# Windowed attention and a gated MLP on one core: q and k by head pair in every batch, token order restored on the read side, V by a plain load and a cast on GpSimd

## The chip, the cores and the metric

The kernel runs on one core of one Trainium2 chip. The metric is device time in microseconds. The engines are named as in the profile: PE (TensorE matmul; PEld is its weight load), DVE (VectorE), ACT (ScalarE), POOL (GpSimd) and SP (SyncE, which here only issues DMAs). SPq, ACTq and POOLq are the sequencers that issue DMAs.

## The reference

Four batches of 8 heads, 768 tokens, head size 64. Attention looks at a causal window of 96 tokens and at the first 8 tokens, with a bias per head that grows with the distance. Its output, as 3072 rows of 512, goes through a SoLU MLP with a layer norm whose scale is `g_ln`.

```python
def attn(q, k, v, n_global, n_local):            # [4, 8, 768, 64], 8, 96
    scores = matmul(q, k.transpose(0, 1, 3, 2)) / sqrt(64)
    rel = pos[:, None] - pos[None, :]
    is_global = pos[None, :] < n_global
    is_local = (rel >= 0) & (rel < n_local)
    dist = where(is_global & ~is_local, n_local, abs(rel))
    scores = where(is_global | is_local, scores - slopes[h] * dist, -1e9)
    return matmul(softmax(scores), v)

def moe(x, w_in, w_out, g_ln):                   # x [3072, 512], d_ff 1024
    h = x @ w_in
    solu = h * softmax(h)
    ln = (solu - mean(solu)) / sqrt(var(solu) + 1e-6) * g_ln
    return ln @ w_out
```

## The kernel before

The 3072 rows are 24 tiles of 128 tokens, six to a batch. One hand-written loop over t = 0 to 28 sets the order of everything, and each engine executes its share of it strictly in that order. In step t the attention of tile t is made, its two head halves as `scores` (PE into PSUM, exp on ACT), `mask_mul` (DVE) and `av` (PE); `norm` (DVE) of tile t-1 ends in `x16`, which PE transposes and DVE copies to `xT`; the MLP of tile t-2 is made up to `u` (PE `ffn_in`, ACT exp, DVE product, then a DMA transpose of `u` issued by SP), ACT squares it, and GpSimd works out the layer-norm statistics for two tiles at a time; `ffn_out` of tile t-4 runs on PE, and ACT scales and stores tile t-5. So the product u of tile n is made in step n+2, and its start marks that step in the trace.

PSUM is full and nothing in it is double-buffered: the tags are s (scores), av, h (`ph`), o (`po`) and t, which the transposes of x, q and k share.

The scores need q and k with the head size on the partitions, so PE transposes them, and the result is copied from PSUM to `qkT` (fp16, one buffer per batch, two buffers).

Batch 0 comes tile by tile: `load_tile0` loads q, k and v of 128 tokens in rows of 256 B, `cast_tile0` casts q and k on ACT and v on GpSimd, and `fill_tile` transposes eight 128x128 blocks and copies them on DVE at L175. This happens inside the loop, in step t for tile t+1. `cast_tile0` also issues the loads of the weights `w_in` (L83) and `w_out` (L85) from GpSimd.

Batches 1 to 3 come by head pair: `load_pair` loads two heads of q or k of the whole batch in rows of 1536 B, which puts six successive tokens on each partition; `cast_pair` casts on GpSimd; `fill_pair` makes six transposes, whose PSUM result has the tokens in the order (a, t) with token = 6t + a. The DVE copy at L188 reads that in order and scatters it on the write side: successive elements of a partition are written 12 B apart. A list FILLS says in which step each of the 8 fills of a batch is made: the last step or steps before the batch that needs them. In batches 1 and 2 the six steps have 2, 1, 1, 2, 1 and 1 fills; in batch 0 they have 0, 0, 1, 2, 2 and 3.

V of batches 1 to 3 comes by DMAs that GpSimd issues and that cast on the way (`load_v`, L91).

The loads of the pairs and the transposes of u are issued by SP, in program order: a load that waits for a free `raw` buffer (8 of them, released by `cast_pair`) holds up the transposes behind it.

The output weights are centred once: `gw_round` (8 ACT instructions) in step 2, then 8 matmuls for a mean and 8 DVE instructions (`gw_centre`, L361) in step 3.

Of the kernel before, what the change touches and what calls it, by code (L numbers as in the profile page):

```python
# [20 lines left out]
def kernel(  # L21
# [45 lines left out]
    st0 = {}  # L67

    def load_tile0(a):
        t = sb.tile([P, 3, H, D], FP32, name="st0", bufs=3)  # L70
        for w, src in enumerate((q, k, v)):
            nc.sync.dma_start(out=t[:, w],
                              in_=src[0, :, ts(a, P), :].rearrange("h p d -> p h d"))
        st0[a] = t

    def cast_tile0(a):
        t = st0.pop(a)
        qk = sb.tile([P, 2, H, D], FP16, name="qk0")
        nc.scalar.copy(out=qk.rearrange("p w h d -> p (w h d)"),  # L79
                       in_=t[:, 0:2].rearrange("p w h d -> p (w h d)"))  # L80
        nc.gpsimd.tensor_copy(out=vo[:, 0, a, :, 0:D], in_=t[:, 2])
        if a == 0:
            nc.gpsimd.dma_start(out=w_in_sb, in_=moe_w_in.rearrange("(j p) f -> p j f", p=P))  # L83
        if a == 1:
            nc.gpsimd.dma_start(out=w_out32,  # L85
                                in_=moe_w_out.rearrange("(j p) c -> p j c", p=P))
            nc.gpsimd.dma_start(out=g_sb, in_=moe_g_ln.rearrange("(j p) -> p j", p=P))
        return qk

    def load_v(b, a):  # L90
        nc.gpsimd.dma_start(out=vo[:, b, a, :, 0:D],  # L91
                            in_=v[b, :, ts(a, P), :].rearrange("h p d -> p h d"))
# [17 lines left out]
    with tc.manual_schedule():  # L110
        for a in range(3):
            load_tile0(a)
# [42 lines left out]
        nc.gpsimd.memset(nhalf, -0.5)  # L155
        meanw = const.tile([P, P], FP16, name="meanw")
# [4 lines left out]
        def fill_tile(a):  # L161

            if 0 not in qkT:
                qkT[0] = sb.tile([P, 2 * NP, S], FP16, name="qkT")
            qk = cast_tile0(a)
            if a + 3 < NA:
                load_tile0(a + 3)
            pt = psum.tile([P, 2 * NP, P], FP16, name="pt", tag="t")
            for w in range(2):
                for pr in range(NP):  # L170
                    nc.tensor.transpose(  # L171
                        out=pt[:, w * NP + pr, :],
                        in_=qk[:, w, 2 * pr : 2 * pr + 2, :].rearrange("p m d -> p (m d)"),
                        identity=ident)
            nc.vector.tensor_copy(out=qkT[0][:, :, ts(a, P)], in_=pt)  # L175

        def fill_pair(b, w, pr):

            if b not in qkT:
                qkT[b] = sb.tile([P, 2 * NP, S], FP16, name="qkT")  # L180
            pt = psum.tile([P, NA, P], FP16, name="pt", tag="t")
            src = qkn.pop((b, w, pr))
            for a in range(NA):
                nc.tensor.transpose(  # L184
                    out=pt[:, a, :],
                    in_=src[:, a].rearrange("p m d -> p (m d)"),
                    identity=ident)
# [99 lines left out]
        def ffn_exp(n):  # L287
            if n % GT == 0:
                sts[n // GT] = [stat.tile([P, GT], FP32, name=f"s{m}") for m in range(3)]
# [3 lines left out]
                                 accum_out=sts[n // GT][0][:, i : i + 1])  # L293

        def ffn_u(n):
# [5 lines left out]
                accum_out=sts[n // GT][1][:, i : i + 1])  # L301
# [4 lines left out]
        def ffn_sq(n):  # L306
# [15 lines left out]
            t2 = stat.tile([P, GT], FP32, name="t2")
            gp.tensor_scalar(out=t2, in0=s2, scalar1=1.0 / D_FF, scalar2=None, op0=ALU.mult)
            gp.tensor_tensor(out=t1, in0=t1, in1=t2, op=ALU.add)
            gp.tensor_scalar(out=t3, in0=t3, scalar1=1e-6, scalar2=None, op0=ALU.mult)
            gp.tensor_tensor(out=t3, in0=t3, in1=t1, op=ALU.add)  # L326
# [20 lines left out]
        def gw_round():  # L347

            t = const.tile([P, NFC, D_MODEL], FP16, name="gw_r")
            for j in range(NFC):  # L350
                nc.scalar.activation(out=t[:, j, :], in_=w_out32[:, j, :],
                                     func=AF.Copy, scale=g_sb[:, j : j + 1])
            return t

        def gw_centre(t):
            pm = psum.tile([P, D_MODEL], FP32, name="pm", tag="o")
            for j in range(NFC):
                nc.tensor.matmul(out=pm, lhsT=meanw, rhs=t[:, j, :],
                                 start=(j == 0), stop=(j == NFC - 1))
            for j in range(NFC):  # L360
                nc.vector.scalar_tensor_tensor(  # L361
                    out=gw_sb[:, j, :], in0=w_out32[:, j, :], scalar=g_sb[:, j : j + 1],
                    in1=pm, op0=ALU.mult, op1=ALU.subtract)

        def has(n):
# [4 lines left out]
        FILLS = [(NA * b + x, (b + 1, f % 2, f // 2)) for b in range(B - 1)  # L370
                 for f, x in enumerate((0, 0, 1, 2, 3, 3, 4, 5) if b else
                                       (2, 3, 3, 4, 4, 5, 5, 5))]

        fill_tile(0)
        for t in range(NT + LAG + 1):
            b, a = divmod(t, NA)
            for tf, what in FILLS:
                if (tf - 4 if tf >= NA else 1 + (tf > 3)) == t:
                    load_pair(*what)
            casts = [what for tf, what in FILLS if (tf - 1 if tf >= NA else tf) == t]  # L380
# [5 lines left out]
            if t >= 3 and t + 4 < NT:  # L386
                for n in ((NA, t + 4) if t == 3 else (t + 4,)):
                    load_v(*divmod(n, NA))
            if casts and b:
# [24 lines left out]
            if t == 2:  # L414
                gwr = gw_round()
            if t == 3:
# [41 lines left out]
```

## Time and profile before

| | us |
|---|---|
| median of 3 runs | 244.37 |
| lowest and highest run | 242.93, 247.04 |
| the profiled execution, its own time | 245.42 |
| its span in the trace | 243.6 |
| what lies around the span | 1.8 |

The profile is that of one execution. Times in the trace are microseconds from the start of the span; "idle before" names what ended the idle time in front of an instruction. A row of a window view gives, for each engine, the busy time and in brackets the number of instructions, then the granted clock of TensorE as a fraction of full speed, the busy share of the DMA engines, and the rate of the transfers.

### The profile page before, as it was taken

Reading aid. Unit: us, or ns where it says so; the run is one execution under the profiler, and the core shown is the slowest. Engines: PE = TensorE matmul, PEld = TensorE weight load, DVE = VectorE, ACT = ScalarE, POOL = GpSimd, SP = SyncE. Lnnn points to the kernel's source line nnn. Section 1 sums busy time; section 2 is a strip of 40 time slices with the busy share of each in tenths; the row PEclk is TensorE's granted clock in tenths of the full one; section 3 lists DMA queues with packets and bytes.
Section 4 is the critical chain, followed back from the end, with each engine's and each line's share of the span. In section 5 each row is a group of like instructions: output and inputs, shape, how many; then the busy total and the mean of one; then the engine's idle time right before and its main releaser. Section 6 shows DMA issues by size and latency. Waiting matters only on the chain.

```text
span 243.6 us, 3661 instructions
## 1 busy us (share of the span) xinstructions
PE 159.5 (65%) x1384; PEld 83.2 (34%) x1384; DVE 160.0 (66%) x208; ACT 128.1 (53%) x199; POOL 89.3 (37%) x196
## 2 busy tenths in 40 slices
PE   0240682461686527598859875988598798989753
PEld 0120441231442213344434443444354344444321
DVE  0130438269758468789988988899888876765300
ACT  5641329550352501457635763677367588877531
POOL 6500116033322491008544391284523525334030
PEclk9999999596577965979997999799989999999979
DMA  7999999905615476317964899168266944334532
GB/s 153 213 267 311 216 279 280 198 1 127 112 24 153 62 179 82 78 73 172 200 148 67 185 211 146 50 103 108 43 94 91 120 103 106 99 87 129 73 102 86
DMA packets 73874, 32.49 MB, mean 133 GB/s; under 512 B 63616, under 2 KB 69760, under 8 KB 73856
## 3 DMA queue, kind: packets, MB, share of 16 engines
q1 hardware_dynamic: 50592, 20.45, 39.5%
q0 software_dynamic: 19808, 5.51, 19.8%
q10 hardware_dynamic: 3456, 6.29, 7.1%
q8 instruction: 11, 0.18, 0.3%
q14 instruction: 7, 0.06, 0.1%
HBM read 23.07 MB, written 6.29 MB: 121 GB/s over the span
## 4 chain that ended last, share of the span: by engine, by line
PE 27%; DVE 24%; ACT 7%; issue 3%; POOL 2%; DMA 1%; ACTq 0%; DVEq 0%; POOLq 0%
DVE qkT L188 16%; PE ph L281 9%; PE po L337 8%; DVE u L298 5%; ACT e L292 4%; PE pt L184 3%; PE pav L243 3%; DVE x L262 2%; PE ps L203 2%; PE pt L269 2%; ACT sq L309 2%; DVE eb L228 1%; ACT osb L343 1%; DMA out_dram<-osb 1%; POOL t L326 1%
## 5 line engine op out<-in xcount | busy, mean ns | idle before, releaser
L188 DVE COPY qkT<-pt 128x768 f16<-128x768 f16 x24 | 65.4, 2723 | 13.7 <-PE pt L184 13.4
L211 ACT ACTIVATE eb<-ps 128x1024 f16<-128x1024 f32 x40 | 40.8, 1019 | 36.2 <-PE ps L203 36.1
L281 PE MATMUL ph<-w_in_sb,xT 128*128 128x512 f16 x192 | 58.5, 459 | 0.6 <-DVE u L298 0.6
L337 PE MATMUL po<-gw_sb,uT 128*128 128x512 f16 x192 | 46.9, 388 | 3.5 <-ACT osb L343 3.5
L292 ACT ACTIVATE e<-ph 128x1024 f16<-128x1024 f32 x24 | 24.6, 1024 | 33.2 <-PE ph L281 32.4
L298 DVE SCALAR_TENSOR_TENSOR u<-e,ph 128x1024 f16<-128x1024 f16 x24 | 29.2, 1218 | 10.5 <-ACT e L292 8.6
L184 PE MATMUL pt<-ident,qkn 128*128 128x128 f16 x144 | 13.2, 233 | 31.3 <-DVE qkT L188 23.5
L228 DVE TENSOR_TENSOR eb<-eb,mask 128x1024 f16<-128x1024 f16 (+1 forms) x48 | 31.9, 665 | 1.3 <-ACT eb L211 1.2
L309 ACT ACTIVATE sq<-u 128x1024 f16<-128x1024 f16 x24 | 25.4, 1057 | 11.5 <-DVE u L298 11.5
L281 PEld LDWEIGHTS <-xT 128*128 128x128 f16 x192 | 20.1, 113 | 25.5 <-issue 13.0
L337 PEld LDWEIGHTS <-uT 128*128 128x128 f16 x192 | 17.7, 99 | 22.7 <-issue 4.6
L171 PE MATMUL pt<-ident,qk 128*128 128x128 f16 x48 | 6.2, 310 | 29.0 <-ACT qk L79 27.3
L221 POOL COPY qkT<-qkT 128x32 f16<-128x32 f16 x16 | 3.4, 210 | 54.7 <-PE ps L203 54.7
L243 PE MATMUL pav<-vo,eb 128*128 128x65 f16 x352 | 20.5, 200 | 3.9 <-DVE eb L228 2.1
L184 PEld LDWEIGHTS <-qkn 128*128 128x128 f16 x144 | 10.4, 104 | 36.5 <-issue 23.8
L250 POOL COPY vo<-vo 8x520 f16<-8x520 f16 x16 | 9.8, 611 | 33.3 <-PE pav L243 33.3
L175 DVE COPY qkT<-pt 128x1024 f16<-128x1024 f16 x6 | 4.2, 692 | 26.5 <-PE pt L171 26.5
L203 PE MATMUL ps<-qkT 64*128 64x128 f16 x352 | 19.8, 234 | 1.4 <-DVE qkT L175 0.8
L105 POOL CAST qkn<-raw 128x768 f16<-128x768 f32 x24 | 19.9, 839 | 2.3 <-issue 2.2
L343 ACT ACTIVATE osb<-po,rs 128x512 f32<-128x512 f32 x24 | 16.3, 680 | 5.5 <-PE po L337 3.5
L317 POOL TENSOR_TENSOR t<-s 128x2 f32<-128x2 f32 x12 | 6.5, 541 | 31.2 <-DVE u L298 31.2
L243 PEld LDWEIGHTS <-eb 128*128 128x128 f16 x352 | 14.2, 101 | 10.5 <-DVE eb L228 3.9
(48 smaller groups left out, 160.8 us busy)
## 6 DMA issues: line engine op xcount, KB each, us to landing
out_dram<-osb ACTq DMA_DIRECT2D x24, 256.0 KB, 2.2
raw<-in_q_dram SPq DMA_DIRECT2D x12, 384.0 KB, 4.0
raw<-in_k_dram SPq DMA_DIRECT2D x12, 384.0 KB, 4.1
vo<-in_v_dram POOLq DMA_DIRECT2D x18, 128.0 KB, 4.6
w_out<-in_moe_w_out_dram POOLq DMA_DIRECT2D x1, 2048.0 KB, 12.4
st<-in_q_dram SPq DMA_DIRECT2D x6, 256.0 KB, 5.0
st<-in_k_dram SPq DMA_DIRECT2D x6, 256.0 KB, 6.2
st<-in_v_dram SPq DMA_DIRECT2D x6, 256.0 KB, 5.2
```

What stands on the lines that cost most here:

```text
L105: nc.gpsimd.tensor_copy(out=t.rearrange("p a m d -> p m a d"), in_=raws.pop((b, w, pr)).rearrange("p m (a d) -> p m a d", d=D))
L184: nc.tensor.transpose(out=pt[:, a, :], in_=src[:, a].rearrange("p m d -> p (m d)"), identity=ident)
L188: nc.vector.tensor_copy(out=qkT[b][:, w * NP + pr, :].rearrange("p (t a) -> p a t", a=NA), in_=pt)
L203: nc.tensor.matmul(out=ps[:, m, slot, blk, :], lhsT=qkT[b][r, NP + pr, ts(a - blk, P)], rhs=qkT[b][r, pr, ts(a, P)], start=True, stop=True)
L211: nc.scalar.activation(out=eb_f, in_=ps.rearrange("p m s b f -> p (m s b f)"), func=AF.Exp, scale=inv_sqrt_d)
L228: nc.vector.tensor_tensor(out=eb.rearrange(pat), in0=eb.rearrange(pat), in1=mk.rearrange(pat if n % NA else "p m s f -> p (m s f)"), op=AL ...
L243: nc.tensor.matmul(out=pav[:, half, ds(i * (D + 1), D + 1)], lhsT=eb[:, m, slot, blk, :], rhs=vo[:, b, a - blk, 4 * half + i, :], start=(i ...
L281: nc.tensor.matmul(out=ph[:, ds(fh * 512, 512)], lhsT=xT[:, j, :], rhs=w_in_sb[:, j, ds(fh * 512, 512)], start=(j == 0), stop=(j == NCC - 1))
L292: nc.scalar.activation(out=es[n], in_=phs[n], func=AF.Exp, accum_out=sts[n // GT][0][:, i : i + 1])
L298: nc.vector.scalar_tensor_tensor(out=u, in0=es.pop(n), scalar=1.0, in1=phs.pop(n), op0=ALU.mult, op1=ALU.mult, accum_out=sts[n // GT][1][: ...
L309: nc.scalar.activation(out=sq, in_=us.pop(n), func=AF.Square, accum_out=sts[n // GT][2][:, i : i + 1])
L337: nc.tensor.matmul(out=po, lhsT=uT[:, c, :], rhs=gw_sb[:, c, :], start=(c == 0), stop=(c == NFC - 1))
```

## The change

Batch 0 comes by head pair like the others. Its 8 loads are issued first (with V of tiles 0 and 1 between and behind them), its casts go to GpSimd, and its 8 fills are made ahead of step 0 (four) and in step 0 behind the first scores (four), with the PSUM tags t and o in turn.

In `fill_pair` the copy now writes `qkT` in order and reads PSUM with a stride: the six values of a run lie 256 B apart. For q it is a DVE copy, for k an ACT copy.

V of every tile is loaded by SP without a cast into one of four buffers, four steps ahead, and cast by GpSimd two steps ahead; `vo` is no longer written by a DMA. The weight loads are issued by GpSimd behind the casts of batch 0.

The fills of batch 1 move one or two steps earlier (steps 1, 2, 3, 3, 4, 4, 5, 5), their loads to steps 0 and 1, and `raw` gets 10 buffers. Every cast of a pair is made a step ahead of its fill.

`gw_round` is split over steps 2 and 3, the mean and `gw_centre` go to step 4. The statistics on GpSimd shrink from eight instructions for two tiles to five, with the factor 1/1024 moved into the ACT square.

```diff
-            nc.vector.tensor_copy(
-                out=qkT[b][:, w * NP + pr, :].rearrange("p (t a) -> p a t", a=NA),
-                in_=pt)
+            dst = qkT[b][:, w * NP + pr, :].rearrange("p (t a) -> p t a", a=NA)
+            (nc.scalar.copy if w else nc.vector.tensor_copy)(
+                out=dst, in_=pt.rearrange("p a t -> p t a"))
...
+    def load_v(n):
+        b, a = divmod(n, NA)
+        vst[n] = sb.tile([P, H, D], FP32, name="vst", bufs=4)
+        nc.sync.dma_start(out=vst[n],
+                          in_=v[b, :, ts(a, P), :].rearrange("h p d -> p h d"))
+    def cast_v(n):
+        b, a = divmod(n, NA)
+        nc.gpsimd.tensor_copy(out=vo[:, b, a, :, 0:D], in_=vst.pop(n))
...
-        t = sb.tile([P, 2, NA * D], FP32, name="raw", bufs=8)
+        t = sb.tile([P, 2, NA * D], FP32, name="raw", bufs=10)
...
+        PAIRS = [(w, pr) for pr in range(NP) for w in range(2)]
+        for i, (w, pr) in enumerate(PAIRS):
+            load_pair(0, w, pr)
+            if i == 3:
+                load_v(0)
+        load_v(1)
...
-                                       (2, 3, 3, 4, 4, 5, 5, 5))]
-        fill_tile(0)
+                                       (1, 2, 3, 3, 4, 4, 5, 5), PAIRS)]
+        def fills0(half):
+            for i, (w, pr) in enumerate(PAIRS[4 * half : 4 * half + 4]):
+                fill_pair(0, w, pr, tag="to"[i % 2])
+        for i, (w, pr) in enumerate(PAIRS):
+            cast_pair(0, w, pr)
+            if i == 3:
+                cast_v(0)
+                fills0(0)
+            if i == 6:
+                nc.gpsimd.dma_start(out=w_in_sb, ...)
+        nc.gpsimd.dma_start(out=w_out32, ...)
+        nc.gpsimd.dma_start(out=g_sb, ...)
+        cast_v(1)
+        load_v(2)
+        load_v(3)
         for t in range(NT + LAG + 1):
...
-                if (tf - 4 if tf >= NA else 1 + (tf > 3)) == t:
+                if max(tf - 4, 0) == t:
                     load_pair(*what)
+            if has(t + 4):
+                load_v(t + 4)
             if has(t):
                 scores(t, 0)
+            if t == 0:
+                fills0(1)
             if has(t - 1):
                 av(t - 1, 1)
                 norm(t - 1)
+            if has(t + 2):
+                cast_v(t + 2)
...
+            if t in (2, 3):
+                for j in range(4 * t - 8, 4 * t - 4):
+                    gw_round(j)
+            if t == 4:
+                gw_mean()
...
+            if t == 4:
+                for j in range(NFC):
+                    gw_centre(j)
```

## Rows read from the trace of the kernel before

**Rows 1.** The page, busy time and share of each engine.

```profile
PE 159.5 (65%) x1384; PEld 83.2 (34%) x1384; DVE 160.0 (66%) x208; ACT 128.1 (53%) x199; POOL 89.3 (37%) x196
```

**Rows 2.** The page, the chain that ended last, shares by line.

```profile
DVE qkT L188 16%; PE ph L281 9%; PE po L337 8%; DVE u L298 5%; ACT e L292 4%; PE pt L184 3%; PE pav L243 3%; DVE x L262 2%; PE ps L203 2%; PE pt L269 2%; ACT sq L309 2%; DVE eb L228 1%; ACT osb L343 1%; DMA out_dram<-osb 1%; POOL t L326 1%
```

**Rows 3.** Windows between starts of u: two steps without fill, one fill, two fills.

```profile
192.70:203.68 10.98, 9.88 (x96) 4.94 (x93) 7.43 (x16) 8.99 (x15) 3.87 (x11) 1.00 0.70 118
...
155.65:162.22 6.57, 5.40 (x60) 2.83 (x56) 6.11 (x8) 4.77 (x8) 4.72 (x12) 1.00 0.31 80
145.40:155.65 10.25, 7.39 (x64) 3.56 (x61) 9.33 (x10) 4.38 (x8) 2.09 (x4) 0.83 0.82 117
```

**Rows 4.** Windows from u(0) to u(4), to u(16), to the end.

```profile
98.70:192.70 94.00, 73.06 (x687) 37.90 (x686) 84.86 (x100) 56.37 (x85) 42.27 (x88) 0.93 0.67 120
37.02:98.70 61.68, 32.77 (x256) 17.86 (x257) 42.33 (x47) 24.19 (x37) 22.75 (x41) 0.72 0.58 119
192.70:243.60 50.90, 40.33 (x327) 19.16 (x323) 24.41 (x46) 32.82 (x51) 13.78 (x40) 0.97 0.46 98
```

**Rows 5.** Timeline: the second fill of a step with two.

```profile
150.39 0.49 PE L184 MATMUL pt<-ident,qkn 128*128 128x128 f16 x6 [2.86 <-DVE qkT L188]
```

**Rows 6.** Timeline of the start: last GpSimd set-up instruction, and a load issued by SP.

```profile
4.74 0.48 POOL L157 MEMSET meanw<- 128x128 f16 x1
...
9.87 10.05 SPq L72 DMA_DIRECT2D st<-in_q_dram  x1
```

**Rows 7.** Waits of SP's queue: us in total, times, longest.

```profile
SPq L98 <- POOL qkn L105: 40.0, 4, 16.5
```

**Rows 8.** Waits, same columns: PE for GpSimd's copy of V rows.

```profile
PE pav L243 <- POOL vo L250: 1.6, 2, 0.8
```

**Rows 9.** Groups by line and form: busy us, mean ns, idle before.

```profile
L188 DVE COPY qkT<-pt 128x768 f16<-128x768 f16 x24 | 65.4, 2723 | 13.7 <-PE pt L184 13.4
L211 ACT ACTIVATE eb<-ps 128x1024 f16<-128x1024 f32 x40 | 40.8, 1019 | 36.2 <-PE ps L203 36.1
...
L105 POOL CAST qkn<-raw 128x768 f16<-128x768 f32 x24 | 19.9, 839 | 2.3 <-issue 2.2
...
L91 POOL DMA_DIRECT2D vo<-in_v_dram x18 | 16.7, 930 | 0.0
L262 DVE TENSOR_TENSOR x<-pav,rl 128x512 f16<-128x512 f32 x24 | 16.6, 692 | 1.1
...
L271 DVE COPY xT<-pt 128x512 f16<-128x512 f16 x24 | 10.2, 423 | 10.7 <-PE pt L269 10.1
...
L258 DVE RECIPROCAL rl<-pav 128x8 f32<-128x8 f32 x24 | 6.4, 265 | 6.1 <-PE pav L243 6.1
...
L361 DVE SCALAR_TENSOR_TENSOR gw_sb<-w_out,g_sb,pm 128x512 f16<-128x512 f32 x8 | 5.4, 743 | 0.0
L351 ACT ACTIVATE gw_r<-w_out,g_sb 128x512 f16<-128x512 f32 x8 | 5.0, 706 | 0.0
L214 ACT ACTIVATE eb<-ps 128x512 f16<-128x512 f32 x8 | 4.8, 596 | 16.6 <-PE ps L203 16.6
...
L175 DVE COPY qkT<-pt 128x1024 f16<-128x1024 f16 x6 | 4.2, 692 | 26.5 <-PE pt L171 26.5
...
L81 POOL CAST vo<-st 128x512 f16<-128x512 f32 x6 | 3.7, 619 | 15.8 <-DMA st<-in_v_dram 15.7
...
L153 POOL MEMSET vo<- 128x192 f16 x1 | 0.9, 940 | 0.0
```

**Rows 10.** DMA issues: KB each, median us from issue to landing.

```profile
w_out<-in_moe_w_out_dram POOLq DMA_DIRECT2D x1, 2048.0 KB, 12.4
...
w_in_sb<-in_moe_w_in_dram POOLq DMA_DIRECT2D x1, 1024.0 KB, 10.2
```

**Rows 11.** Windows of 2 us: tile loads alone; later, with pair loads under way.

```profile
8.00:10.00 2.00, 0.60 (x6) 0.61 (x7) 0.00 (x0) 1.34 (x3) 0.11 (x1) 1.00 1.33 216
...
40.00:42.00 2.00, 0.00 (x0) 0.00 (x0) 1.95 (x3) 2.00 (x5) 2.00 (x4) 1.00 1.06 381
```

More of the change, by code (lines that the diff above doesn't have):

```diff
@@ L65 @@
     gw_sb = const.tile([P, NFC, D_MODEL], FP16, name="gw_sb")
[L67 to L92, printed above, removed]
+    vst = {}
+    def load_v(n):
[6 more added lines that the diff above has]
+        nc.gpsimd.tensor_copy(out=vo[:, b, a, :, 0:D], in_=vst.pop(n))
     raws, qkn = {}, {}
     def load_pair(b, w, pr):
-        t = sb.tile([P, 2, NA * D], FP32, name="raw", bufs=8)
+        t = sb.tile([P, 2, NA * D], FP32, name="raw", bufs=10)
         nc.sync.dma_start(
@@ L155 @@
         nc.gpsimd.memset(nhalf, -0.5)
+        coef = const.tile([P, 2, GT], FP32, name="coef")
+        nc.gpsimd.memset(coef[:, 0], 1e-6)
+        nc.gpsimd.memset(coef[:, 1], -1.0 / (float(D_FF) * float(D_FF)))
         meanw = const.tile([P, P], FP16, name="meanw")
@@ L159, with fill_pair @@
         qkT = {}
[L161 to L177, printed above, removed]
+        def fill_pair(b, w, pr, tag="t"):
             if b not in qkT:
                 qkT[b] = sb.tile([P, 2 * NP, S], FP16, name="qkT")
-            pt = psum.tile([P, NA, P], FP16, name="pt", tag="t")
+            pt = psum.tile([P, NA, P], FP16, name="pt", tag=tag)
             src = qkn.pop((b, w, pr))
@@ L288, in ffn_exp @@
             if n % GT == 0:
-                sts[n // GT] = [stat.tile([P, GT], FP32, name=f"s{m}") for m in range(3)]
+                sts[n // GT] = stat.tile([P, 3, GT], FP32, name="st")
             i = n % GT
@@ L345, in store @@
             nc.scalar.dma_start(out=out[ts(n, P), :], in_=osb)
-        def gw_round():
-            t = const.tile([P, NFC, D_MODEL], FP16, name="gw_r")
-            for j in range(NFC):
[L351 to L358, printed above, removed]
+        gw_r = const.tile([P, NFC, D_MODEL], FP16, name="gw_r")
@@ L359, in gw_centre, with gw_round, gw_mean @@
+        pms = []
+        def gw_round(j):
+            nc.scalar.activation(out=gw_r[:, j, :], in_=w_out32[:, j, :],
+                                 func=AF.Copy, scale=g_sb[:, j : j + 1])
+        def gw_mean():
+            pms.append(psum.tile([P, D_MODEL], FP32, name="pm", tag="o"))
+            for j in range(NFC):
+                nc.tensor.matmul(out=pms[0], lhsT=meanw, rhs=gw_r[:, j, :],
                                  start=(j == 0), stop=(j == NFC - 1))
[L360 to L363, printed above, removed]
+        def gw_centre(j):
+            nc.vector.scalar_tensor_tensor(
+                out=gw_sb[:, j, :], in0=w_out32[:, j, :], scalar=g_sb[:, j : j + 1],
+                in1=pms[0], op0=ALU.mult, op1=ALU.subtract)
@@ L375 @@
+        nc.gpsimd.dma_start(out=g_sb, in_=moe_g_ln.rearrange("(j p) -> p j", p=P))
+        cast_v(1)
+        load_v(2)
+        load_v(3)
         for t in range(NT + LAG + 1):
@@ L385 @@
                 norm(t - 1)
[L386 to L389, printed above, removed]
+            if has(t + 2):
+                cast_v(t + 2)
+            if casts:
                 cast_pair(*casts.pop(0))
             if has(t):
-                if b == 0 and a + 1 < NA:
-                    fill_tile(a + 1)
                 mask_mul(t, 0)
+            if t in (2, 3):
[3 more added lines that the diff above has]
+                gw_mean()
             if has(t - LAG - 1):
@@ L413 @@
                 cast_pair(*what)
-            if t == 2:
-                gwr = gw_round()
-            if t == 3:
-                gw_centre(gwr)
+            if t == 4:
+                for j in range(NFC):
+                    gw_centre(j)
             if has(t - LAG):
```

37 lines of the change are left out of this document (16 added, 21 removed).

## The prediction

> **What bounds the kernel now.** I read the busy shares first: DVE and PE stand level at about 160 us of 243.6 [rows 1], so no engine is full and the question is who waits for whom. The chain that ended last names one line above all others, the DVE copy L188 that scatters the transposed q and k into `qkT` [rows 2]; its 24 instructions take 2.72 us each, where the copy L175 moves a third more elements in 0.69 us [rows 9]. Its price is seen by cutting the trace from one start of u to a later one. Two successive steps without a fill take 10.98 us, so 5.5 us each, a step with one fill 6.57 and a step with two 10.25 [rows 3]. A single 2.72 us copy is mostly hidden behind the matmuls of the step. Two are not: both use the one PSUM tag t, so PE stands 2.86 us in front of the second set of transposes [rows 5], and the granted clock of that step is 0.83, where the other two steps have 1.00 [rows 3]. Without fills PE is busy 9.88 of 10.98 us [rows 3]; that is the floor under the steps.
>
> The span falls into four stages: 37.0 us to u(0), 61.7 to u(4), 94.0 to u(16), 50.9 to the end [rows 4]. The third is six steps each of batches 1 and 2, 16 fills, and the last has none. The second, four steps with seven fills and the centring of the output weights, is far from any floor: PE is busy 32.8 us of 61.7, at a mean granted clock of 0.72 [rows 4].
>
> **The change part by part. The copy.** Sixteen copies go to DVE and sixteen to ACT, in place of 24 plus 6. Element by element the writes are now in order and the PSUM reads jump 256 B. No row shows a DVE or ACT copy whose successive PSUM reads jump. The only such read is the reciprocal L258, 8 elements 260 B apart in 265 ns on average, too few to tell a rate. From below: DVE takes 423 ns for 512 and 692 ns for 1024 fp16 elements in order, so 0.53 ns each above 154 ns, and 768 would take 0.56 us. At the rate of L262, (692 - 154) / 512 = 1.05 ns, they take 0.96 us; on ACT L214 and L211 give 0.83 ns above 173, so 0.81 us. From above: if the jump costs on the read side what it costs now on the write side, 2.72 us; by the slowest strided row, the GpSimd memset L153 at 940 / 192 = 4.9 ns, 3.76 us [rows 9]. I take 0.96 on DVE and 0.81 on ACT, since L262 is a DVE read of PSUM at the slower of the two rates that PSUM reads show, and nothing in the rows says that the read side is what L188 pays for.
>
> [...] L188 crosses SBUF in 12 B steps at (2723 - 154) / 768 = 3.3 ns per element [rows 9]. [...]
>
> **Steps with one fill.** The 1.05 us between 6.57 and 5.5 become the six transposes, 0.5 us [rows 5]; the copy is hidden by scores, av and `ffn_in` on PE. A k copy stands on ACT ahead of the next exp, but ACT is busy only 4.5 us of a 5.5 us step [rows 3]. I take 6.0. Should that cover go, it costs up to 0.8.
>
> **Steps with two fills.** PE waits for one copy, the q copy on DVE: 5.5 + 0.5 + 0.9 + 0.5 = 7.4, without a drop of the clock. The wait that is late next there is the same one, shorter.
>
> **u(4) to u(16).** Eight steps with one fill and four with two: 8 x 6.0 + 4 x 7.4 = 77.6 in place of 94.0.
>
> **u(0) to u(4).** The fills of batch 1 now stand 1, 1, 2, 2, 2 in steps 1 to 5, so 6.0 + 3 x 7.4 = 28.2 for the four steps in between. To that come half of `gw_round`, 4 x 0.71 = 2.8 us on ACT, of which I expose 2; `gw_centre`, 8 x 0.74 = 5.9 at most on DVE in step 4, of which I expose 4, its mean matmuls 2; and the clock: PE's 32.8 busy us at 0.72 hold 23.6 us at full clock, and of the 9 between I keep 3.5, since the long waits go. Sum 39.7 in place of 61.7. In both kernels this holds the same casts on GpSimd, 0.84 us per pair [rows 9]. What goes is SP's wait for `raw` buffers, 40.0 us in four waits [rows 7], behind which transposes of u stood; with 10 buffers and casts a step ahead I price what is left at nothing, covered by the four steps between the making of u and its use, and at up to a few us if a cast comes late.
>
> **The start.** GpSimd's set-up ends at 5.2 [rows 6], plus two small memsets 6.0. Four casts of pairs at 0.84 end at 9.4, and transposes and copy of the last put the first scores at 11. The cast of V(0), 0.62 [rows 9], three more casts and one DMA issue put the `w_out` issue at 14.3, `w_in` about two microseconds before; the last fill of batch 0 ends at 16. So far this is no bound. The weights land 10.2 and 12.4 us after their issue [rows 10]; now `w_out` lands at 14.3 + 12.4 = 26.7, then the first half of `gw_round` (2.8, in front of the exp of tile 0 on ACT) and that exp with its wait make u(0) start at 31. Between: 27 if the longer rows (216 GB/s with tile loads alone, 381 later with pair loads under way [rows 11]) let it land in half the time, 38 if all behind it queues. SP's ten-microsecond issue of a 256 B-row load with full queues [rows 6] goes with these loads, though V keeps such rows.
>
> **V and GpSimd.** 18 DMA issues at 0.93 us become 18 casts at 0.62 [rows 9], two steps ahead of their use, behind the copy of the global rows; this hides, with GpSimd at 37% [rows 1], and its cost if it did not would be 0.6 per step. SP gets 24 V loads in front of its transposes of u, covered by the same four steps. The shorter statistics can give back PE's waits for V rows behind them, 1.6 us in two places [rows 8]; I take 1 off the last stage: 49.9.
>
> **Sum.** 31 + 39.7 + 77.6 + 49.9 + 1.8 around the span = 200.0, against the execution's own 245.42. The median of the runs is 0.4% lower, so 199.
>
> **Rivals.** First, the first batch stays held up. Its casts all stand on GpSimd now, and weights, batch 1 and V share the queues. Against it: up to u(4) about 13 MB must come in, batch 0 with q, k and v 4.7, weights 4.2, batch 1's pairs 3.1 and V about 1, which is 61 us at 216 and 34 at 381 GB/s [rows 11], both under the 70.7 that I give the two stages. For it: weights land after casts. With u(0) at 38 and 50 us for the next stage: 38 + 50 + 77.6 + 49.9 + 1.8 = 217, 216 by the median.
>
> Second, the jump costs as much on the read side, 2.72 us on both engines. The late wait stays in steps with two fills, 10.3 each, and a step with one becomes 6.9, as ACT then carries 4.5 + 2.7 in every other: 8 x 6.9 + 4 x 10.3 = 96.4. The stage before: 6.9 + 3 x 10.3 + 11.5 = 49.3; the start 33; the sum with 50 and 1.8 is 230.5, by the median 229. The gain is then the first batch alone.
>
> Third, both of these: 229 and the 17 that the first rival adds are 246, no change. That would also be the case in which the change doesn't do what it says, DVE's time being given back elsewhere.
>
> Fourth, slower: a strided PSUM read dearer than the strided write, at 3.76 us. Each further 1.04 us is paid once per fill in stages two and three and in the start: 23 fills and four in a row make 28 us, so 257. It decides from about 3.4 us per copy. For it only the far row of GpSimd; against it that L258 reads PSUM across 260 B in 265 ns in all.
>
> **How the numbers follow.** The forecast case has 0.58, with a range of its own of 187 to 210; the first rival 0.18 (208 to 226), the second 0.14 (222 to 238), the third 0.06, the fourth 0.04. A measurement here tells about 2% from no change. Faster: 0.58 + 0.18 + 0.14 = 0.90; same 0.06; slower 0.04. For 8 in 10 the range takes the forecast case, the first rival and the lower half of the second, so 185 to 230; its lower end is also where copies at 0.56 us and an early `w_out` lead.
>
> **What would show it.** In the profile after: fill copies of about 0.96 us on DVE and 0.81 on ACT; two-fill steps near 7.4 us with a granted clock of 1.00; u(0) at 31, u(4) at 71, u(16) at 148; PE above 75% busy and the chain led by PE. The forecast is wrong if a copy takes over 2 us, if u(0) comes after 38, or if ACT's queue (a k copy waiting for transposes behind `ffn_out`) leads the chain.

## The result, and the profile after

The changed kernel takes 203.48 us (median of 4 runs, 202.88 to 205.57), the kernel before, run beside it, 244.82 (4 runs, 242.93 to 247.04): a ratio of 0.835, 95% interval [0.826, 0.844]. The profiled execution has 202.88 us of its own, a span of 201.1 and so 1.8 around it. Ratios here and below leave out runs that show a second, slower state of the core; the profiles of three experiments (late pairs, fills first, both) come from such runs, and only their steps and waits are used.

The starts of u(0), u(4) and u(16) cut the span after at 37.54, 78.26 and 152.50 us. The window view of the four stages, then of single steps in the third: one q fill, one k fill, two fills.

```profile
0.00:37.54 37.54, 17.13 (x148) 10.60 (x149) 10.59 (x19) 16.39 (x33) 18.59 (x39) 0.96 1.01 288
37.54:78.26 40.72, 27.16 (x228) 14.33 (x228) 25.60 (x40) 22.56 (x35) 17.40 (x32) 0.79 0.61 143
78.26:152.50 74.24, 66.88 (x692) 37.75 (x691) 54.79 (x93) 60.45 (x93) 35.66 (x71) 1.00 0.79 177
152.50:201.10 48.60, 37.62 (x319) 18.29 (x317) 24.52 (x45) 32.52 (x51) 12.21 (x30) 1.00 0.40 105
...
85.38:90.85 5.47, 5.20 (x58) 2.97 (x57) 4.53 (x8) 4.67 (x8) 3.80 (x8) 1.00 0.53 117
127.91:134.08 6.17, 5.82 (x62) 3.20 (x60) 4.09 (x8) 5.37 (x9) 3.66 (x7) 1.00 0.75 138
134.08:141.23 7.15, 5.42 (x63) 3.20 (x62) 5.34 (x9) 5.48 (x9) 4.10 (x9) 1.00 0.50 126
```

| stage, us | before [rows 4] | predicted | after | gain |
|---|---|---|---|---|
| start to u(0) | 37.0 | 31 | 37.5 | -0.5 |
| u(0) to u(4) | 61.7 | 39.7 | 40.7 | 21.0 |
| u(4) to u(16) | 94.0 | 77.6 | 74.2 | 19.8 |
| u(16) to the end | 50.9 | 49.9 | 48.6 | 2.3 |

The gain lies in the second and third stage in nearly equal parts. Most of the last stage's 2.3 us is not the change's: 1.9 of it stands behind the last u, and there the granted clock differs. Before, the stretch takes 13.2 us at 0.87; the same code takes there 11.7 at 0.99 in the run below that changes the copy's direction alone; the changed kernel takes 11.3 at 1.00.

```profile
230.41:243.60 13.19, 5.67 (x18) 1.90 (x16) 1.23 (x2) 3.10 (x5) 2.09 (x8) 0.87 0.36 109
...
198.87:210.60 11.73, 4.15 (x18) 1.55 (x16) 1.23 (x2) 3.10 (x5) 2.09 (x8) 0.99 0.33 104
...
189.77:201.10 11.33, 4.14 (x18) 1.54 (x16) 1.23 (x2) 3.10 (x5) 1.48 (x5) 1.00 0.32 96
```

A q fill now costs a step nothing (5.47 us against 5.5 without a fill [rows 3]), a step with two fills 7.15 in place of 10.25, and the granted clock in it is 1.00, not 0.83.

From the page: the busy shares, and the chain by engine and line.

```profile
PE 148.8 (74%) x1384; PEld 81.0 (40%) x1384; DVE 115.5 (57%) x194; ACT 131.9 (66%) x209; POOL 83.9 (42%) x170
...
ACT 34%; DVE 20%; PE 16%; DMA 16%; issue 6%; SPq 3%; ACTq 3%; POOL 1%; DVEq 0%; POOLq 0%
DVE u L274 14%; ACT e L268 13%; DMA g_sb<-in_moe_g_ln_dram 9%; ACT eb L186 6%; PE ph L256 6%; ACT osb L314 5%; ACT sq L285 5%; DMA raw<-in_q_dram 4%; DVE qkT L164 3%; ACTq L316 3%; PE po L308 3%; ACT gw_r L323 2%; DVE eb L203 2%; PE pt L160 2%; DMA raw<-in_k_dram 2%
```

The copy, first in the chain before [rows 2], is at 3%; the chain is now that of the MLP (exp, product u), led by ACT, and 9% of it is the load of the norm scale `g_sb`, issued behind the output weights. The groups of the fill copies and the casts:

```profile
L164 DVE COPY qkT<-pt 128x768 f16<-128x768 f16 x16 | 15.3, 955 | 14.1 <-PE pt L160 13.9
L164 ACT COPY qkT<-pt 128x768 f16<-128x768 f16 x16 | 12.7, 793 | 20.0 <-PE pt L160 20.0
L77 POOL CAST vo<-vst 128x512 f16<-128x512 f32 x24 | 15.6, 656 | 8.9 <-DMA vst<-in_v_dram 8.9
```

Two holes are left. The first is at the start (timeline of GpSimd and ACT, with the DMA issues; columns start, duration):

```profile
15.62 0.91 POOL L358 DMA_DIRECT2D w_out<-in_moe_w_out_dram  x1
...
33.94 2.56 ACT L323 ACTIVATE gw_r<-w_out,g_sb 128x512 f16<-128x512 f32 x4 [5.41 <-DMA g_sb<-in_moe_g_ln_dram]
```
```profile
w_out<-in_moe_w_out_dram POOLq DMA_DIRECT2D x1, 2048.0 KB, 17.9
```

`w_out` is issued at 15.6 and lands 17.9 us later; ACT waits 5.41 us for it and its scale, in front of the exp of tile 0. The DMA engines are busy nearly throughout (mean share 1.01 in the first window above). The second hole is in step 4:

```profile
56.97 5.35 DVE L333 SCALAR_TENSOR_TENSOR gw_sb<-w_out,g_sb,pm 128x512 f16<-128x512 f32 x8
...
62.37 3.25 PE L308 MATMUL po<-gw_sb,uT 128*128 128x512 f16 x8 [7.50 <-DMA raw<-in_k_dram]
...
67.53 0.80 ACT L164 COPY qkT<-pt 128x768 f16<-128x768 f16 x1 [9.90 <-PE pt L160]
...
71.01 1.89 PE L308 MATMUL po<-gw_sb,uT 128*128 128x512 f16 x8
```

PE stands 7.50 us in front of the first output product and ACT 9.90 us in front of a k copy whose transposes are queued on PE behind that product; the step takes 16.2 us. After the wait the eight matmuls of the product take 3.25 us, at a granted clock of 0.57, and 1.89 in the next step. The name that the trace gives as releaser, a load of k, can't be it: the product starts as the eight centring instructions on DVE end (56.97 + 5.35 = 62.32), and it reads what they write.

### The profile page after: what moved, and what is told of

It reads as the page before. It is cut to its first block, busy times and chain, and to the rows that moved or that the text cites. A ratio compares the mean times of both kernels' runs of the same rounds, so it can differ in the third digit from the quotient of the medians.

```text
span 201.1 us, 3648 instructions
## 1 busy us (share of the span) xinstructions
PE 148.8 (74%) x1384; PEld 81.0 (40%) x1384; DVE 115.5 (57%) x194; ACT 131.9 (66%) x209; POOL 83.9 (42%) x170
## 4 chain that ended last, share of the span: by engine, by line
ACT 34%; DVE 20%; PE 16%; DMA 16%; issue 6%; SPq 3%; ACTq 3%; POOL 1%; DVEq 0%; POOLq 0%
DVE u L274 14%; ACT e L268 13%; DMA g_sb<-in_moe_g_ln_dram 9%; ACT eb L186 6%; PE ph L256 6%; ACT osb L314 5%; ACT sq L285 5%; DMA raw<-in_q_dram 4%; DVE qkT L164 3%; ACTq L316 3%; PE po L308 3%; ACT gw_r L323 2%; DVE eb L203 2%; PE pt L160 2%; DMA raw<-in_k_dram 2%
## 5 line engine op out<-in xcount | busy, mean ns | idle before, releaser
L256 PE MATMUL ph<-w_in_sb,xT 128*128 128x512 f16 x192 | 48.6, 399 | 0.6 <-DVE u L274 0.6
L186 ACT ACTIVATE eb<-ps 128x1024 f16<-128x1024 f32 x40 | 40.7, 1017 | 7.1 <-PE ps L178 7.1
L203 DVE TENSOR_TENSOR eb<-eb,mask 128x1024 f16<-128x1024 f16 (+1 forms) x48 | 37.4, 779 | 7.5 <-ACT eb L186 4.1
L160 PE MATMUL pt<-ident,qkn 128*128 128x128 f16 x192 | 18.8, 245 | 19.5 <-DVE qkT L164 9.9
L90 POOL CAST qkn<-raw 128x768 f16<-128x768 f32 x32 | 26.8, 838 | 7.6 <-DMA raw<-in_q_dram 5.0
L164 ACT COPY qkT<-pt 128x768 f16<-128x768 f16 x16 | 12.7, 793 | 20.0 <-PE pt L160 20.0
L160 PEld LDWEIGHTS <-qkn 128*128 128x128 f16 x192 | 14.2, 109 | 25.6 <-POOL qkn L90 11.6
L225 POOL COPY vo<-vo 8x520 f16<-8x520 f16 x16 | 11.7, 733 | 29.1 <-PE pav L218 28.9
L164 DVE COPY qkT<-pt 128x768 f16<-128x768 f16 x16 | 15.3, 955 | 14.1 <-PE pt L160 13.9
L293 POOL TENSOR_TENSOR t<-st 128x4 f32<-128x4 f32 x12 | 6.6, 547 | 34.5 <-DVE u L274 34.5
L218 PEld LDWEIGHTS <-eb 128*128 128x128 f16 x352 | 14.3, 101 | 12.7 <-DVE eb L203 9.1
L77 POOL CAST vo<-vst 128x512 f16<-128x512 f32 x24 | 15.6, 656 | 8.9 <-DMA vst<-in_v_dram 8.9
L178 PEld LDWEIGHTS <-qkT 64*128 64x128 f16 x352 | 11.1, 98 | 18.6 <-issue 9.5
## 6 DMA issues: line engine op xcount, KB each, us to landing
w_out<-in_moe_w_out_dram POOLq DMA_DIRECT2D x1, 2048.0 KB, 17.9
```

Source lines behind the costliest of these rows:

```text
L90: nc.gpsimd.tensor_copy(out=t.rearrange("p a m d -> p m a d"), in_=raws.pop((b, w, pr)).rearrange("p m (a d) -> p m a d", d=D))
L160: nc.tensor.transpose(out=pt[:, a, :], in_=src[:, a].rearrange("p m d -> p (m d)"), identity=ident)
L164: (nc.scalar.copy if w else nc.vector.tensor_copy)(out=dst, in_=pt.rearrange("p a t -> p t a"))
L178: nc.tensor.matmul(out=ps[:, m, slot, blk, :], lhsT=qkT[b][r, NP + pr, ts(a - blk, P)], rhs=qkT[b][r, pr, ts(a, P)], start=True, stop=True)
L186: nc.scalar.activation(out=eb_f, in_=ps.rearrange("p m s b f -> p (m s b f)"), func=AF.Exp, scale=inv_sqrt_d)
L203: nc.vector.tensor_tensor(out=eb.rearrange(pat), in0=eb.rearrange(pat), in1=mk.rearrange(pat if n % NA else "p m s f -> p (m s f)"), op=AL ...
```

## The experiments

Theory: the gain is the direction of the copy (an in-order SBUF write and a jumping PSUM read), in every fill; the rest of the change, the new first batch above all, adds what is left. Rivals: the split of the copies over two engines makes the gain, or the first batch alone does. Then come tests of the two holes. Ratios are to the kernel before; the changed kernel has 0.835 [0.826, 0.844].

**Stride back on the write side, all else changed.**

```diff
-            dst = qkT[b][:, w * NP + pr, :].rearrange("p (t a) -> p t a", a=NA)
-            (...)(out=dst, in_=pt.rearrange("p a t -> p t a"))
+            dst = qkT[b][:, w * NP + pr, :].rearrange("p (t a) -> p a t", a=NA)
+            (...)(out=dst, in_=pt)
```


> The kernel after, with the stride of the fill copy put back on the write side, q still on DVE and k on ACT. Theory (the direction of the stride is the gain of the stage u(4) to u(16)): DVE copies 2.72 us again, ACT copies also well over 2 us, the stage goes from 74 back to about 92 to 96 us, total about 225 to 232. Rival (splitting the copies over two engines and the earlier casts are the gain): the stage stays within 4 us of 74, total 203 to 210. If only DVE pays for strided writes, ACT copies stay at 0.8 us and the total is about 212 to 218.

Measured 242.29 us, 0.990 [0.987, 0.995]: nearly the whole gain is gone, more than expected. Its groups show what the jumping write costs, the same on either engine:

```profile
L164 ACT COPY qkT<-pt 128x768 f16<-128x768 f16 x16 | 43.7, 2730 | 31.5 <-PE pt L160 31.5
L164 DVE COPY qkT<-pt 128x768 f16<-128x768 f16 x16 | 43.4, 2715 | 13.4 <-PE pt L160 13.3
```

u(4) to u(16) takes 99.9 us, more than before (94.0). The k copies, now on ACT, which also makes the exps, cost most: a step with one k fill takes 7.7 to 8.0 us, one with a q fill 6.1 to 6.3. u(0) to u(4) takes 52.6 in place of 61.7, so the rest of the change wins 9.1 us there, but only 2.3 us in all (244.6 beside it): alone, the first batch is not the gain.

**Only the copy's direction changed, in the kernel before.**

```diff
-                out=qkT[b][:, w * NP + pr, :].rearrange("p (t a) -> p a t", a=NA),
-                in_=pt)
+                out=qkT[b][:, w * NP + pr, :].rearrange("p (t a) -> p t a", a=NA),
+                in_=pt.rearrange("p a t -> p t a"))
```


> The kernel before with nothing changed but the direction of the copy: strided PSUM read, write in order, all on DVE. Theory: copies 0.96 us, u(4) to u(16) from 94 to about 74 to 77, u(0) to u(4) from 62 to about 50, start and end as they were; total 214 to 220, so about two thirds of the whole gain. Rival (the rest of the change makes the gain possible): u(0) to u(4) stays near 60 and total 224 or more.

Measured 212.12 us, 0.865 [0.859, 0.871], two us under the expected range. The windows u(0) to u(4), u(4) to u(16) and to the end:

```profile
36.19:89.39 53.20, 31.18 (x263) 17.39 (x261) 28.97 (x47) 24.19 (x37) 23.11 (x41) 0.74 0.67 136
89.39:161.16 71.77, 65.97 (x690) 37.52 (x689) 59.28 (x100) 55.04 (x85) 43.17 (x87) 1.00 0.88 157
161.16:210.60 49.44, 38.31 (x322) 18.60 (x320) 24.32 (x45) 32.75 (x51) 14.79 (x42) 1.00 0.48 102
```

Two lines of source make some 32 of the 41 us (244.6 beside it, less 212.1), and all that the third stage gains, 71.8 there being better than the changed kernel's 74.2. On top of it the rest of the change is worth the 8.6 us between 212.1 and 203.5, in the second stage (53.2 to 40.7). There direction alone gains 8.5 us, the rest alone 9.1, and both together 21.0, 3.4 more than the sum. The split over two engines and the way of V, tested below, are by their medians worth about 2 us of it at most; what is left (first batch, earlier casts with more `raw` buffers, the rounding and centring in other steps, shorter statistics) no run takes apart. One lead is SP's wait for casts of pairs: 40.0 us before [rows 7], in this run and then in the changed kernel

```profile
SPq L98 <- POOL qkn L105: 35.7, 5, 17.4
...
SPq L83 <- POOL qkn L90: 0.3, 1, 0.3
```

**All copies on DVE.**

```diff
-            (nc.scalar.copy if w else nc.vector.tensor_copy)(
-                out=dst, in_=pt.rearrange("p a t -> p t a"))
+            nc.vector.tensor_copy(out=dst, in_=pt.rearrange("p a t -> p t a"))
```


> The kernel after with all 32 fill copies on DVE, reads strided as now. Theory (direction is the gain, the split is not): copies 0.96 us, the steps with a k fill alone, 5.8 to 6.2 us now, fall to about 5.5 and steps with two fills stay near 7.1, total 199 to 204. Rival (the split is the gain, DVE becomes late again): each step with two fills grows by about 1 us and steps with one k fill stay, total 206 to 212.

Measured 203.03 us, 0.829 [0.826, 0.832]; the intervals overlap, so the split over two engines is not the gain. u(4) to u(16) is even 2.2 us shorter (72.0), which comes back in the last run below. In the profiled execution the last stage gives that back, behind the last u, at a granted clock of 0.75:

```profile
186.79:200.70 13.91, 6.70 (x18) 2.07 (x16) 1.23 (x2) 3.10 (x5) 1.48 (x5) 0.75 0.26 78
```

**Copy in order on both sides.** It leaves out the restoring of the token order, so the outputs' values are others.

```diff
-            dst = qkT[b][:, w * NP + pr, :].rearrange("p (t a) -> p t a", a=NA)
-            (...)(out=dst, in_=pt.rearrange("p a t -> p t a"))
+            dst = qkT[b][:, w * NP + pr, :].rearrange("p (a t) -> p a t", a=NA)
+            (...)(out=dst, in_=pt)
```


> The kernel after, but the fill copies read PSUM in order and write in order; this leaves out the restoring of the token order, so q and k are attended in a permuted order. It measures what the strided read itself costs. [...] Total 199 to 203 by either.

One run, 203.52 us. Its groups, to be read against the 793 and 955 ns above:

```profile
L164 ACT COPY qkT<-pt 128x768 f16<-128x768 f16 x16 | 12.6, 791 | 17.8 <-PE pt L160 17.8
L164 DVE COPY qkT<-pt 128x768 f16<-128x768 f16 x16 | 8.9, 554 | 15.3 <-PE pt L160 15.2
```

Jumping 256 B in PSUM costs ACT nothing (793 against 791 ns) and DVE 0.40 us (955 against 554), and no time of the kernel that a single run can tell. The two jumps differ in distance as well as in side (12 B on the SBUF write, 256 B on the PSUM read), and no run tried either distance on the other side.

**Loads of batch 1 later.**

```diff
-                if max(tf - 4, 0) == t:
+                if max(tf - (4 if tf >= NA else 2), 0) == t:
```


> The kernel after, with the loads of batch 1's pairs issued two steps ahead of their fill instead of up to four: 2, 2, 2 and 2 loads in steps 0 to 3 in place of 6 and 2 in steps 0 and 1. Theory (the start is bound by the bytes in front of the output weights, the DMA engines being fully busy to 37.5 us at 288 GB/s; 1.6 MB less in front is about 5 us): u(0) from 37.5 to 32 to 34, total 198 to 201. Rival (the place of gw_round on ACT or the casts on GpSimd hold u(0), not the bytes): u(0) at 36 or later, total 202 to 205.

Measured 203.42 us, 0.830 [0.822, 0.837]. `w_out` lands 17.1 us after its issue (17.9 in the changed kernel), and u(0) starts at 37.7.

```profile
w_out<-in_moe_w_out_dram POOLq DMA_DIRECT2D x1, 2048.0 KB, 17.1
...
0.00:37.66 37.66, 16.61 (x148) 10.45 (x149) 10.75 (x18) 16.36 (x33) 20.29 (x42) 1.00 0.99 277
```

Putting the loads off gains nothing, but it is a weak test of the bytes: at 277 GB/s 10.4 MB have come in up to u(0), 10.8 in the changed kernel, so some 0.4 MB went out of the way and not the 1.6 that were meant.

**Weights issued first**, behind the second cast of batch 0 (the lines that issued them later are taken out).

```diff
+            if i == 1:
+                nc.gpsimd.dma_start(out=w_in_sb, ...)
+                nc.gpsimd.dma_start(out=w_out32, ...)
+                nc.gpsimd.dma_start(out=g_sb, ...)
```


> The kernel after, with the three weight loads issued by GpSimd behind the first two casts of batch 0 instead of behind the seventh and eighth, about 7 us earlier. Theory (the weights come late because of when they are issued and what stands in the other queue by then): the output weights land at 24 to 28 us in place of 33.8, u(0) at 32 to 35, total 198 to 202. Rival (the start is bound by the sum of the bytes, whatever their order): the pairs and V of batch 0 come later by what the weights gain, u(0) within 1.5 us of 37.5, total 202 to 206.

Measured 202.78 us, 0.829 [0.825, 0.834]. The weights are issued 8 us earlier and have landed by 25.5; u(0) starts at 36.6 all the same. The timeline of SP and GpSimd shows what waits in their place:

```profile
7.75 14.41 SPq L72 DMA_DIRECT2D vst<-in_v_dram  x3
...
17.84 0.83 POOL L90 CAST qkn<-raw 128x768 f16<-128x768 f32 x1 [2.92 <-DMA raw<-in_k_dram]
...
22.21 3.14 SPq L83 DMA_DIRECT2D raw<-in_q_dram  x1
...
25.86 0.93 POOL L77 CAST vo<-vst 128x512 f16<-128x512 f32 x1 [7.20 <-DMA vst<-in_v_dram]
...
29.18 0.83 POOL L90 CAST qkn<-raw 128x768 f16<-128x768 f32 x1 [1.61 <-DMA raw<-in_q_dram]
```

Now the last pair of batch 0 and V of tile 1 come late. The chain into u(0) runs through a load that tile 0 doesn't need: the first pair of batch 1 is issued at 22.2, behind the V loads, and its cast stands on GpSimd in front of a copy for the next scores. So the order in the queues of SP and GpSimd is in the way as well as the transfers, and no run separates the two.

**All of the rounding in step 3**, behind the exp of tile 0.

```diff
-            if t in (2, 3):
-                for j in range(4 * t - 8, 4 * t - 4):
+            if t == 3:
+                for j in range(NFC):
```


> The kernel after, with all eight gw_round instructions in step 3 instead of four each in steps 2 and 3, so that the exp of tile 0 no longer stands behind the landing of the output weights on ACT. Rival to the bytes (the order on ACT is the whole delay): u(0), u(1) and u(4) all come about 5 us earlier, total 197 to 200. Theory (the bytes): u(0) comes at 32 to 33, but V of tile 4 and batch 1's pairs land no earlier, so u(1) stays at 42 or later and the total at 201 to 204.

Measured 205.18 us, 0.840 [0.835, 0.845]. u(0) comes at 31.9, 5.7 us earlier, but u(1) at 46.4 where the changed kernel has 45.0: ACT stands 4.50 us for the scores of the next tile and then makes all eight roundings (4.99 us) in a row.

```profile
37.33 0.61 POOL L77 CAST vo<-vst 128x512 f16<-128x512 f32 x1 [8.81 <-DMA vst<-in_v_dram]
...
39.46 1.02 ACT L186 ACTIVATE eb<-ps 128x1024 f16<-128x1024 f32 x1 [4.50 <-PE ps L178]
40.38 4.99 ACT L323 ACTIVATE gw_r<-w_out,g_sb 128x512 f16<-128x512 f32 x8
```

The scores wait for a copy on GpSimd, and that stands behind the cast of V of tile 4, which is needed two steps later. Taking the wait for `w_out` out of the start gains nothing while V of batch 0 still comes in and is cast in that place.

**Centring spread over two steps**, the output products of tiles 0 to 2 made up for in steps 5 and 6.

```diff
-            if t == 4:
-                for j in range(NFC):
+            if t in (4, 5):
+                for j in range(4 * t - 16, 4 * t - 12):
...
+            if t == 5:
+                ffn_out(0)
+            elif t == 6:
+                ffn_out(2)
```
with `store(0)` and `ffn_out(1)` ahead in step 6.

> The kernel after, with gw_centre split, four instructions in step 4 and four in step 5, and the first output products moved: ffn_out of tile 0 to the end of step 5, tile 1 to step 6 behind the store of tile 0, tile 2 to the end of step 6. Theory (the 7.5 us wait of PE in step 4 is for gw_centre on DVE, with fills and scores queued behind ffn_out): u(2) to u(3) falls from 16.2 to 9 to 11 us, later steps grow by 3 in sum, total 199 to 202. Rival (the wait is for the k load that the profile names): u(2) to u(3) stays at 14 or more, total 203 to 206.

Measured 210.19 us, 0.861 [0.856, 0.866], a miss: 6.7 us slower than the changed kernel where a gain was expected. Timeline of PE:

```profile
60.55 0.80 PE L160 MATMUL pt<-ident,qkn 128*128 128x128 f16 x6 [5.39 <-DVE qkT L164]
...
71.35 3.57 PE L308 MATMUL po<-gw_sb,uT 128*128 128x512 f16 x8 [4.86 <-DVE gw_sb L333]
...
79.06 3.44 PE L308 MATMUL po<-gw_sb,uT 128*128 128x512 f16 x8 [1.40 <-ACT osb L314]
```

One hole of 7.5 us became two of some 5: each half stands on DVE in front of a fill copy or of the product, and two output products, not one, run at the lower rate (3.4 to 3.6 us for eight matmuls, and 1.89 later).

**V of batches 1 to 3 by GpSimd's casting DMA**, as before.

```diff
-            if has(t + 4):
+            if has(t + 4) and t + 4 < NA:
...
-            if has(t + 2):
+            if has(t + 2) and t + 2 < NA:
...
+            if t + 4 < NT and t + 4 >= NA:
+                nc.gpsimd.dma_start(out=vo[:, bv, avn, :, 0:D], in_=...)
```


> The kernel after, with V of batches 1 to 3 loaded as in the kernel before (DMA issued by GpSimd, casting on the way), four steps ahead. It undoes the V part alone. Theory (V's way in is off the path): total 202 to 205, steps unchanged. Rival (GpSimd's issue of 0.93 us and its casting transfers hold the copies of the global rows up): steps grow by 0.3 us each, total 207 to 210.

Measured 205.54 us, 0.841 [0.836, 0.846]; u(4) to u(16) 74.7, the last stage 48.7. So the plain V load with its cast is worth about 1% (2.1 us), if anything: the intervals overlap.

**In step 4 the fills first, then the centring**, then `ffn_out`.

```diff
+                for tf, what in FILLS:
+                    if tf == t:
+                        fill_pair(*what)
                 for j in range(NFC):
                     gw_centre(j)
...
-                if tf == t:
+                if tf == t and t != 4:
```


> The kernel after, with the order turned round at the end of step 4: both fills, then gw_centre, then ffn_out of tile 0. Theory (PE's 7.5 us wait is for gw_centre on DVE, and the fills queue behind it): the fills move under that wait, u(2) to u(3) from 16.2 to 13.5 to 14.5 us, total 201 to 202. Rival (a load or a transfer is waited for): u(2) to u(3) stays within 0.7 of 16.2.

Measured 0.830 [0.825, 0.836], the same. u(2) to u(3) is 14.8 us in place of 16.2, and the wait now shows its true name, which settles the releaser that the profile after named wrongly:

```profile
66.56 3.23 PE L308 MATMUL po<-gw_sb,uT 128*128 128x512 f16 x8 [4.77 <-DVE gw_sb L333]
```

**Fills first, and the centring in fp16.** The mean is copied to fp16 once and subtracted from `gw_r`, already rounded, in four instructions of 1024 in place of eight of 512 in fp32; the rounding differs slightly.

```diff
-                for j in range(NFC):
-                    gw_centre(j)
+                nc.vector.tensor_copy(out=pm16, in_=pms[0])
+                for j in range(0, NFC, 2):
+                    nc.vector.tensor_tensor(out=gw_sb[:, j : j + 2, :],
+                        in0=gw_r[:, j : j + 2, :], in1=pm_b, op=ALU.subtract)
```
(`pm_b` reads `pm16` twice; the fills as in the run above.)

> As the run with the fills first, and the centring made from the rounded weights: one copy of the mean to fp16 and four DVE subtractions of 1024 elements with all operands fp16 in SBUF, in place of eight instructions of 512 with fp32 operands. The rounding of the centred weights differs slightly. Theory (DVE's 5.35 us there are on the path): DVE time 0.4 + 4 x 0.70 = 3.2 us, u(2) to u(3) at 11 to 12.5 us, total 198.5 to 200.5. Rival (not on the path): as the run with the fills first, within 0.5 us.

Measured 199.05 us (198.83 to 202.89), 0.814 [0.810, 0.818]: 2.2% below the changed kernel's median, and its interval ends below where that kernel's begins. The timeline of DVE and PE in step 4:

```profile
57.61 0.68 DVE L334 CAST pm<-pm 128x512 f16<-128x512 f32 x1
58.32 2.50 DVE L338 TENSOR_TENSOR gw_sb<-gw_r,pm 128x1024 f16<-128x1024 f16 x4
59.06 3.02 PE L308 MATMUL po<-gw_sb,uT 128*128 128x512 f16 x8 [0.71 <-DVE gw_sb L338]
```

3.2 us on DVE do what 5.35 did, and the product begins at the first piece. u(2) to u(3) falls to 10.7 us, 5.5 less. The end comes 4.1 us earlier (spans of 201.1 and 197.0): u(0) is 1.3 later in this execution, so u(0) to u(4) is 34.0 in place of 40.7, and the last stage is 50.0 at a clock of 0.97 where it was 48.6 at 1.00.

**That, and all copies on DVE.** The edits of both runs together.

> The version with the fills first and the fp16 centring, and in addition all fill copies on DVE. Theory (a k copy on ACT stands in front of the next exp, and the ACT steps are the slower ones: 6.17 us against 5.47 for a DVE step; with all copies on DVE u(4) to u(16) took 72.0 us against 74.2): u(4) to u(16) 72 us, no step with one fill above 5.8, total 196.5 to 198. Rival (the two copies of a two-fill step, now in a row on DVE, and DVE's centring and copies in steps 4 and 5 give the gain back, and the 51.2 us of the last stage in that run belongs to it): u(4) to u(16) 72 to 74, last stage 50 to 51 us, total 199 to 201.

Measured 199.03 us (197.96 to 202.41, 6 runs), 0.813 [0.808, 0.817]. The window u(4) to u(16), and a step with one fill:

```profile
77.82:149.83 72.01, 66.05 (x690) 37.43 (x689) 62.02 (x100) 55.12 (x85) 35.57 (x71) 1.00 0.81 180
...
89.99:95.45 5.46, 5.12 (x58) 2.87 (x56) 5.25 (x8) 4.66 (x8) 3.65 (x7) 1.00 1.20 229
```

The theory's steps are there (72.0 us, no step with one fill above 5.8): a k copy on ACT costs a step up to 0.7 us, on DVE at most 0.3. But 2.2 us of one stage are not seen in the medians (199.05 and 199.03; the total lies in the rival's range, and so does the last stage, 50.8), so on the total the run leaves it open. Neither pair of runs shows a gain from the split over two engines.

## Why the prediction was right, point by point

The sign, the cause and the size held: 199 was forecast, 203.5 measured, and the forecast case is the one that came. Of the stages, the first two took 7.5 us more than forecast and the last two 4.7 less, so the sum of 200.0 met 202.9. That it came so near is in part luck: the errors of the stages offset each other, and the 1.3 us by which the last stage came out shorter than forecast lie behind the last u, where the granted clock differs (13.2 us at 0.87 before, 11.3 at 1.00 after).

*The copy.* Taken at 0.96 and 0.81 us, measured 0.955 and 0.793. The step that carried the forecast, that the write side is what L188 pays for, is shown from both ends: with the jump back on the write side a copy takes 2.72 us on either engine, and without any jump ACT takes the same 0.79. The price came from L262's rate, and in-order PSUM reads run at 0.55 us for the same 768 elements on DVE, so the choice of the slower of two rates came out as well, though no row then said that a jump brings it about. The second rival (229), the third (246) and the fourth (257) needed a dear jump on the read side; at 256 B in PSUM there is none (a copy takes 0.955 us on DVE and 0.793 on ACT). The second was also priced too low: the run with the stride back on the write side is its case, 2.7 us on both engines, and takes 242, with u(0) at 39.2 in place of 33 and the next two stages at 52.6 and 99.9 in place of 49.3 and 96.4. By that run, a read as dear as the write would have left no gain to speak of.

*Steps with fills.* One fill: 6.0 predicted, 5.73 on average (45.8 us in eight steps); two: 7.4 predicted, 7.1 on average (28.4 in four), at a clock of 1.00. The stage is 3.4 us shorter than forecast, 2.1 of them because a q fill is hidden altogether (5.47); the k fill on ACT, 5.80 to 6.17 us, is what the prediction feared for it, and the last run shows it.

*The start.* This is the term that was mis-sized: 31 predicted, 37.5 measured, at the far end of its bounds (27 to 38). The issue of `w_out` came at 15.6, near the 14.3 of the working; its landing was taken at 12.4 us from a row of before [rows 10] and took 17.9. Three other orders were tried and none helps: weights first move the wait to V and to pairs, rounding later moves it to the next tile, later pairs change nothing. The DMA engines are busy nearly without a break until u(0) (mean share 1.01), and the prediction had weighed the transfers over the first two stages together, where they fit, and not over the first alone. But that their sum, at 288 GB/s, is the bound is not shown: in two of the three orders the wait that ends last goes through a cast on GpSimd for a later tile or batch that stands in front of work needed at once. Why `w_out` takes 17 to 18 us in all these orders isn't settled.

*u(0) to u(4).* 39.7 predicted, 40.7 measured. In the kernel before, this stage holds eight fills by the list FILLS, not seven, and the change moves four of the fills by one step each, none by two; the sum counts the seven of the changed kernel rightly. Of the 11.5 us that the prediction added to the steps, most stands in one place, step 4 (16.2 us against 7.4), where `gw_centre`, exposed at 4, holds PE for 7.5 and is followed by a product at the low rate (3.25 us for its eight matmuls, 1.89 a step later). The first rival (216) had this stage at 50 and u(0) at 38: the late u(0) came, the long stage did not.

*V and GpSimd, the last stage.* SP's loads of pairs, which waited 40.0 us for casts of pairs before [rows 7], wait 0.3 for them after, so pricing what is left at nothing was right; for GpSimd as a whole SP's loads still wait 15.1 us, 5.7 at the longest. V by plain loads wins about 1%, if anything. The last stage is 48.6, 49.9 predicted: 0.4 us are won up to the last u (37.3 against 37.7) and about as much behind it at a like clock (11.3 against 11.7), near the 1 us that was taken; the rest goes with the clock (13.2 us at 0.87 against 11.7 at 0.99).

*What would show it.* PE was to lead the chain and be above 75% busy; PE is at 74% and ACT leads with 34%. This part was wrong, without consequence for the time: ACT leads by the exps of the MLP and not by a k copy that waits behind `ffn_out`, which is seen once, in step 4, and PE is still busy 5.20 of the 5.47 us of a step with a q fill.

## What to carry to other kernels

Where a copy from PSUM must reorder, try the jump on the read and write SBUF in order; one edit of two lines was over three quarters of this change (a 256 B jump read, 0.96 us on DVE and 0.79 on ACT, for a 12 B jump written, 2.72 and 2.73; other distances weren't run). Cut the trace by a marker that each step has (here the starts of u) and price each kind of step: the dear kind shows what an average over the span hides. Where transfers fill the DMA engines, earlier issue can move a wait and not remove it (here the weights, issued 8 us earlier, brought u(0) from 37.5 to 36.6 us only); look then for a cast or a copy that waits for data of a later tile at the head of an in-order queue. A one-off preparation (here the centring) that stands in front of another engine's queue was better made short (199.05 us, with the fills first) than split over two steps with the products moved (210.19).

## What was not expected of the hardware

A copy of 768 fp16 elements that jumps 12 B on the SBUF write takes 2.72 us on DVE and 2.73 on ACT, 3.5 ns per element; ACT, slower than DVE on the in-order copy (0.79 against 0.55), is no slower here. The same copy with a 256 B jump on the PSUM read costs ACT nothing (793 against 791 ns) and puts DVE from 554 to 955 ns.

The rate of the loads varied: in windows of 4 us with the DMA engines busy nearly throughout, the kernel after moved between 169 and 412 GB/s, the least right behind the issue of three V loads, in 256 B rows, and of the weights.

```profile
14.00:18.00 4.00, 2.40 (x20) 1.55 (x20) 1.29 (x2) 1.60 (x3) 3.99 (x6) 1.00 0.96 169
...
26.00:30.00 4.00, 3.03 (x20) 1.46 (x21) 1.50 (x3) 1.02 (x1) 1.53 (x3) 1.00 1.03 412
```

SP's issue of those three V loads took 6.17 us, from 7.67 on, and 14.41 with the weights ahead of them (shown above), though the first V load, among the first loads of the kernel, was issued in 0.47.

```profile
2.77 0.47 SPq L72 DMA_DIRECT2D vst<-in_v_dram  x1
...
7.67 6.17 SPq L72 DMA_DIRECT2D vst<-in_v_dram  x3
```
